# An S5 scan gated by a GEGLU block on one core: up weights loaded in whole rows, the first slab's up products regrouped, and new orders

## The chip, the cores and the metric

The kernel runs on one core of a Trainium2 chip. The metric is the device time of one execution in microseconds, lower is better. Differences of about 0.3% are at the edge of what a measurement of this kernel can tell.

## The reference

The input x has 2048 tokens of 512 features (bfloat16). It is normalized, and the normalized rows go two ways: through a diagonal state space layer with 512 complex states, and through a GEGLU block with 1376 hidden columns.

```python
xn = _layernorm(x)                       # no scale, no shift
# S5
dt = exp(log_dt); Lam_bar = exp(dt * Lam)
B_bar = ((Lam_bar - 1.0) / Lam)[:, None] * Bmat
Bu = einsum("bld,pd->blp", xn, B_bar)
h[t] = Lam_bar * h[t-1] + Bu[t]          # 2048 steps
s = 2.0 * einsum("blp,dp->bld", h, Cmat).real + xn * Dskip
# GEGLU, silu, gate
g = silu((gelu(xn @ w_gate) * (xn @ w_up)) @ w_down)
out = x + s * g
```

## The kernel before

**Tiling.** The tokens are cut into four slabs of 512, each of four tiles (`m`) of 128. The 512 features are four row tiles (`k`) of 128. The 1376 hidden columns are cut into three chunks (`c`): 0 to 512, 512 to 1024 and 1024 to 1376. `wu`, `wg` and `wd` are the three weights in the on-chip buffer, `x_tok` holds all of x, `xna` the four normalized tiles of a slab, and `xnT` two slabs of them transposed.

**Work of a slab.** The up and gate products (for each tile three chunks of each weight, four matmuls to a chunk, one per row tile) accumulate in banks of PSUM; ScalarE (ACT) evicts them, with a gelu for the gate; VectorE (DVE) multiplies the two (`gated`); a transposing DMA (`at_t`) turns the product, and `down_pair` multiplies it with `wd`, 11 matmuls for each tile. For the scan, `half(s, h)` multiplies `BT` with `xnT` (16 matmuls in four groups), ACT evicts into `U`, and DVE rotates (`rot`, `turn`), runs four scans and rotates back into `hst`. `y_tile` multiplies `hst` with `C2` (8 matmuls for each tile, on top of a skip term that ACT puts into the bank first), and DVE applies the gate and adds x. The last tile's y is done in two halves.

**The first slab is special.** No transposing DMA has run yet, so its tiles are centered (`center`), transposed on TensorE (`head_t`, four transposes per tile, a copy by DVE or ACT into `xcT`, which lies in the buffer `W`), and multiplied as they come. `up_rows(m, k, c)` is one matmul of one tile, one row tile and one chunk; `first_w` is a whole group of four; both are scaled by the row's inverse deviation `rs` when ACT evicts them (`out_up`). The seven matmuls of `dummies` stand ahead of it.

**Banks.** There are eight PSUM banks: six of pool "ps" and two of pool "pp". `bank(part)` takes from "pp" if `part` is true. Before the change the third chunk and all of tile 3 go to "pp".

**What sets the order.** Every instruction group is added to a `Plan` as a step with its dependences. `Plan.run` emits the steps in the order of the tuple `ORDER`, and `SLOTS` gives the buffer of each group of a pool. Each engine, and each DMA queue, runs its own instructions in the order of emission. The costs, landing times and due times that appear as numbers in the calls, such as those of `load_x` and `load_w`, were for the planner that wrote `ORDER` and `SLOTS`; in the kernel they do nothing. Almost all DMAs are issued from SP's queue.

**The loads before.** In `ORDER`, the first DMAs on SP are: three x tiles; `wu` row 0 of chunk 0, then of chunk 1; `wu` chunk 2 of all four rows in one load; `wu` row 1 of chunk 1; the fourth x tile; the rest of `wu` in four loads; `wg` in two loads, columns 512 to 1376 first; the second slab of x; the broadcast of `Dskip`; `BT` of the real part, the first `xnT`, `BT` of the imaginary part.

The lines of the profile that matter below: L287 `load_w`, L291 `load_slab`, L296 `load_x`, L314 the loads of `BT`, L328 small memsets, L356 the statistics of a slab, L387 and L400 the transposes of `head_t`, L402 and L391 the copies to `xcT`, L436 the transposing DMA into `xnT`, L462 `up_rows`, L499 `first_w`, L471 and L505 their evictions, L536 the up and gate products of later slabs, L564 `down_pair`, L579 y, L615 BT times xnT, L617 its eviction, L627, L635 and L639 the rotations, L646 the scans, L838 the sums of later slabs, L843 their normalization.

Of the kernel before, what the change touches and what calls it, by code (L numbers as in the profile page):

```python
# [18 lines left out]


ORDER = (
# [24 lines left out]
)  # L46
SLOTS = {
# [4 lines left out]
    ),  # L52
    "pp": (
        0, 1, 0, 1, 0, 1, 0, 1, 0, 0, 0, 1, 0, 1, 0, 1, 0, 1, 0, 1, 1, 0, 1, 0, 1, 1, 1, 0, 0, 0, 0, 1, 1, 0, 1, 0, 1, 0, 1,
    ),
    "U": (
        0, 1, 0, 2, 0, 1, 0, 2,
    ),
    "g2": (
        5, 0, 1, 4, 3, 0, 4, 2, 2, 0, 1, 5, 3, 1, 4, 5,  # L60
    ),
    "at": (
        2, 0, 1, 3, 2, 1, 0, 0, 0, 1, 2, 3, 2, 3, 0, 1,
    ),
    "gtA": (
        0, 0, 1, 1, 0, 1, 0, 1, 1, 0, 0, 0, 1, 1, 0, 0,
    ),
    "gtB": (
        1, 1, 0, 0, 0, 0, 1, 1, 1, 0, 0, 0, 0, 1, 0, 1,
    ),  # L70
    "ubA": (
        0, 1, 0, 0, 1, 1, 1, 0, 0, 0, 1, 1,
    ),
    "ubB": (
        0, 0, 1, 1, 1, 0, 0, 1, 0, 0, 1, 0,
    ),
    "yg": (
        0, 0, 1, 1, 0, 1, 0, 1, 0, 1, 1, 0, 0, 0, 1, 0, 1, 0,
    ),
    "ot": (  # L80
        1, 1, 1, 0, 1, 0, 0, 0, 0, 0, 0, 1, 1, 0, 1, 0, 1,
    ),
    "sk": (
        2, 3, 0, 1, 5, 7, 4, 6, 0, 1, 3, 2, 5, 4, 6, 7,
    ),
    "atT": (
        0, 1, 3, 0, 1, 1, 3, 2, 0, 3, 2, 1, 1, 2, 3, 0,
    ),
}

# [58 lines left out]
def kernel(  # L149
# [18 lines left out]
    P = 128  # L168
    S = 2048
    D = 512  # L170
    F = 1376
    KT = D // P
# [5 lines left out]
    M = TS // P  # L178
# [3 lines left out]
    CH = [(0, 512), (512, 1024), (1024, F)]  # L182
# [6 lines left out]
    V, A, G, T = nc.vector, nc.scalar, nc.gpsimd, nc.tensor  # L189
# [11 lines left out]
    wg = sb("wg", [P, KT, F])  # L201
    wu = sb("wu", [P, KT, F])
# [10 lines left out]
    W2 = CH[1][1]  # L213
# [32 lines left out]
    def bank(part=False):  # L246
        pool = "pp" if part else "ps"
        g, i = pl.group(pool)
        return (pool, g), banks[SIZES["ps"] + i if part else i]
# [9 lines left out]
    def pe(n, cols, emit, reads=(), writes=(), **kw):  # L259
        return pl.add(PE, n * (cols + 6) / 2400.0, emit, reads, writes, lag=0.22, **kw)  # L260
# [23 lines left out]
    def load_w(nm, k0, k1, c0, c1, end, landed):  # L284

        w, r = w_of[nm]
        dma_sp(end, landed, lambda: nc.sync.dma_start(out=w[:, k0:k1, c0:c1], in_=r[:, k0:k1, c0:c1]),  # L287
               [(nm, k, c) for k in range(k0, k1) for c in range(3) if c0 <= CH[c][0] < c1])
# [6 lines left out]
    def load_x(m, end, landed):  # L295
        dma_sp(end, landed, lambda: nc.sync.dma_start(out=x_tok[:, m, :], in_=x_r[:, m, :]), [("x", 0, m)])  # L296

    W1 = CH[0][1]
    load_x(0, 1.12, 2.92)
    load_x(1, 1.59, 3.35)  # L300
    load_x(2, 2.06, 3.75)
    load_w("wu", 0, 1, 0, W1, 2.53, 4.4)
    load_w("wu", 0, 1, W1, W2, 3.0, 4.95)
    load_w("wu", 1, 2, 0, W1, 3.47, 5.5)
    load_w("wu", 1, 2, W1, W2, 3.94, 6.05)
    load_x(3, 4.41, 6.6)
    load_w("wu", 2, 3, 0, W1, 4.88, 7.15)
    load_w("wu", 2, 3, W1, W2, 5.35, 7.7)
    load_w("wu", 3, 4, 0, W2, 5.82, 8.8)
    load_w("wu", 0, KT, W2, F, 6.29, 10.0)  # L310
    load_w("wg", 0, KT, W1, F, 6.76, 12.4)
    load_w("wg", 0, KT, 0, W1, 7.23, 14.0)
    for ri, src in enumerate((A_B_re, A_B_im)):
        dma(SP, 2.0, 3.0, lambda ri=ri, src=src: nc.sync.dma_start_transpose(out=BT[:, ri, :, :], in_=src), writes=[("BT", ri)],  # L314
            after=list(sp_last), svc=TURN)
# [138 lines left out]
    def up_rows(m, k, c):  # L454

        a, b = CH[c]
        if (m, c) not in opened:
            opened[m, c] = bank(m == 3)
        key, ps = opened[m, c]

        def f():
            T.matmul(ps[:], lhsT=xcT[:, k, m * P : (m + 1) * P], rhs=wu[:, k, a:b], start=(k == 0), stop=(k == KT - 1))  # L462
        pe(1, 512, f, [("xcT", m, k // 2), ("wu", k, c)], [key])
        if k == KT - 1:
            out_up(m, c, ps, key)

# [263 lines left out]
    for m in range(1, M):  # L730
        norms = rstd(m, m + 1)
    head_t(1)
    up_rows(0, 0, 0)
    up_rows(0, 0, 1)
    head_t(2)
    for c in range(2):
        up_rows(1, 0, c)
    up_rows(0, 1, 0)
    up_rows(1, 1, 0)
    for c in range(2):  # L740
        up_rows(2, 0, c)
    for m in range(2):
        up_rows(m, 1, 1)
    for c in range(2):
        up_rows(2, 1, c)
    head_t(3)
    for c in range(2):
        for m in range(3):
            up_rows(m, 2, c)
    for k in range(3):  # L750
        for c in range(2):
            up_rows(3, k, c)
    for m in range(M):
        for c in range(2):
            up_rows(m, 3, c)
    for m in range(M):
        first_w("wu", m, 2)
    for m in range(M):
        first_gates(m)
    load_slab(1, after=sp_last)  # L760
# [159 lines left out]
```

## Time and profile before

| | |
|---|---|
| runs of the kernel | 178.75, 178.93, 179.28 us; median 178.93 |
| span of the profiled execution | 176.9 us |
| instructions in it | 2418 |
| HBM read, written | 6.46 MB, 2.10 MB |

Only the span is given of the profiled execution; its time is not among the three runs. The span runs from its first to its last instruction; the runs' median lies 2.03 us above it. The profile counts an engine as busy while one of its instructions executes; matmuls are pipelined, so a displayed matmul duration contains its latency, and the chain of waits gives the slots in which they follow one another. "SPq" is the queue of SyncE's DMA issues, "PEld" the weight loads, which overlap the matmuls. A row of the timeline is: start, length, engine, line, operation, what it writes from what, and how many; in brackets stands how long its engine idled before it and who ended that.

### The profile page before, as it was taken

Reading aid. Unit: us, or ns where it says so; the run is one execution under the profiler, and the core shown is the slowest. Engines: PE = TensorE matmul, PEld = TensorE weight load, DVE = VectorE, ACT = ScalarE, POOL = GpSimd, SP = SyncE. Lnnn points to the kernel's source line nnn. Section 1 sums busy time; section 2 is a strip of 40 time slices with the busy share of each in tenths; the row PEclk is TensorE's granted clock in tenths of the full one; section 3 lists DMA queues with packets and bytes.
Section 4 is the critical chain, followed back from the end, with each engine's and each line's share of the span. In section 5 each row is a group of like instructions: output and inputs, shape, how many; then the busy total and the mean of one; then the engine's idle time right before and its main releaser. Section 6 shows DMA issues by size and latency. Waiting matters only on the chain.

```text
span 176.9 us, 2418 instructions
## 1 busy us (share of the span) xinstructions
PE 172.1 (97%) x834; PEld 82.3 (47%) x849; DVE 154.6 (87%) x253; ACT 132.6 (75%) x246; POOL 10.9 (6%) x25
## 2 busy tenths in 40 slices
PE   8999999999999999999999999999999999999992
PEld 2554544454454444444444444444444444444451
DVE  3743799999999988999999699999999999999343
ACT  6679999989999999956697665735898860793310
POOL 2640500000200000011000000000000000000000
PEclk9999999999999999999999999999999999999999
DMA  5999999997092730040057050063007300550531
GB/s 150 285 347 247 160 288 189 305 217 158 8 193 43 138 62 4 0 82 0 0 115 150 2 111 0 0 126 70 0 11 154 87 0 4 129 123 0 113 119 30
DMA packets 48467, 18.66 MB, mean 105 GB/s; under 512 B 40296, under 2 KB 48328, under 8 KB 48456
## 3 DMA queue, kind: packets, MB, share of 16 engines
q1 hardware_dynamic: 48432, 18.52, 46.7%
q8 instruction: 6, 0.10, 0.2%
q14 instruction: 5, 0.04, 0.1%
q10 hardware_dynamic: 24, 0.00, 0.0%
HBM read 6.46 MB, written 2.10 MB: 48 GB/s over the span
## 4 chain that ended last, share of the span: by engine, by line
PE 94%; DMA 2%; SPq 1%; issue 1%; DVE 0%
PE bank L536 31%; PE bank L564 21%; PE bank L615 16%; PE bank L579 16%; PE bank L499 7%; PE bank L462 3%; DMA wu<-in_B_w_up_dram 2%; SPq L296 1%; SPq L287 0%; DVE yg L585 0%; DVE ot L586 0%; PE bank L400 0%
## 5 line engine op out<-in xcount | busy, mean ns | idle before, releaser
L536 PEld LDWEIGHTS <-xnT 128*128 128x128 bf16 x288 | 28.1, 98 | 29.4
L564 PE MATMUL bank<-wd,atT 128*128 128x512 bf16 (+1 forms) x174 | 40.2, 379 | 0.1
L536 PE MATMUL bank<-wu,xnT 128*128 128x512 bf16 (+1 forms) x140 | 31.9, 356 | 0.1
L536 PE MATMUL bank<-wg,xnT 128*128 128x512 bf16 (+1 forms) x139 | 31.7, 356 | 0.3
L615 PE MATMUL bank<-xnT,BT 128*128 128x512 bf16 x128 | 30.9, 379 | 0.1
L646 DVE TENSOR_TENSOR_SCAN Fs<-rho,ini,W 128x512 bf16<-128x512 f32 x24 | 29.8, 1272 | 0.1
L579 PE MATMUL bank<-C,hst 128*128 128x512 bf16 (+1 forms) x134 | 29.7, 366 | 0.1
L564 PEld LDWEIGHTS <-atT 128*128 128x128 bf16 (+1 forms) x176 | 17.2, 98 | 20.3
L539 ACT ACTIVATE ubA<-bank 128x512 bf16<-128x512 f32 x24 | 14.6, 614 | 8.8 <-PE bank L536 8.3
L617 ACT ACTIVATE U<-bank 128x512 bf16<-128x512 f32 x32 | 19.1, 622 | 1.7 <-PE bank L615 1.7
L579 PEld LDWEIGHTS <-hst 128*128 128x128 bf16 x136 | 13.3, 98 | 14.0
L615 PEld LDWEIGHTS <-BT 128*128 128x128 bf16 x128 | 12.5, 98 | 14.3
L627 DVE TENSOR_TENSOR Q<-U,tab 128x4096 bf16<-128x4096 bf16 x8 | 18.3, 2287 | 0.7 <-ACT tab L715 0.6
L539 ACT ACTIVATE gtA<-bank 128x512 bf16<-128x512 f32 x24 | 14.8, 616 | 5.3 <-PE bank L536 4.6
L627 DVE TENSOR_TENSOR Q<-Fs,tab 128x4096 bf16<-128x4096 bf16 x8 | 18.3, 2285 | 0.1
L567 ACT ACTIVATE g<-bank 128x512 f32<-128x512 f32 x16 | 9.2, 594 | 12.1 <-PE bank L564 12.1
L585 DVE TENSOR_TENSOR yg<-bank,g 128x512 bf16<-128x512 f32 (+1 forms) x17 | 11.1, 655 | 5.0 <-PE bank L579 4.6
L539 ACT ACTIVATE ubB<-bank 128x352 bf16<-128x352 f32 x12 | 5.7, 475 | 6.6 <-PE bank L536 5.5
L838 ACT ACTIVATE junk<-x_tok 128x512 bf16<-128x512 bf16 x16 | 10.2, 649 | 0.0
L499 PE MATMUL bank<-wg,W 128*128 128x512 bf16 (+1 forms) x47 | 9.7, 356 | 0.1
L843 ACT ACTIVATE xna<-x_tok,nb,rs 128x512 bf16<-128x512 bf16 x12 | 9.6, 876 | 0.0
L575 ACT ACTIVATE bank<-sk 128x512 f32<-128x512 bf16 (+1 forms) x17 | 9.5, 577 | 0.1
(121 smaller groups left out, 190.0 us busy)
## 6 DMA issues: line engine op xcount, KB each, us to landing
out_dram<-ot SPq DMA_DIRECT2D x15, 128.0 KB, 1.8
x_tok<-in_A_x_dram SPq DMA_DIRECT2D x3, 512.0 KB, 5.6
wd<-in_B_w_down_dram SPq DMA_DIRECT2D x1, 1280.0 KB, 7.1
wg<-in_B_w_gate_dram SPq DMA_DIRECT2D x1, 864.0 KB
wu<-in_B_w_up_dram SPq DMA_DIRECT2D x6, 128.0 KB, 3.3
x_tok<-in_A_x_dram SPq DMA_DIRECT2D x4, 128.0 KB, 2.2
wg<-in_B_w_gate_dram SPq DMA_DIRECT2D x1, 512.0 KB, 7.8
wu<-in_B_w_up_dram SPq DMA_DIRECT2D x1, 352.0 KB, 3.9
```

The costliest lines, as they stand in the source:

```text
L499: T.matmul(ps[:, 0 : b - a], lhsT=xcT[:, k, m * P : (m + 1) * P], rhs=wt[:, k, a:b], start=(k == 0), stop=(k == KT - 1))
L536: T.matmul(ps[:, 0 : b - a], lhsT=xnT[:, s % 2, m, k, :], rhs=wt[:, k, a:b], start=(k == 0), stop=(k == KT - 1))
L539: acts(b - a, lambda: act(out=dst, in_=ps[:, 0 : b - a], func=AF.Copy if up else AF.Gelu_apprx_tanh), [key], [ok], table=None if up else " ...
L564: T.matmul(ps[:], lhsT=atT[:fs, k, iT * P : (iT + 1) * P], rhs=wd[:fs, k, :], start=(k == 0), stop=(k == NFT - 1))
L579: T.matmul(ps, lhsT=hst[s % 2][:, j // NPT, j % NPT, m * P : (m + 1) * P], rhs=C2[:, j // NPT, j % NPT, c0:c1], start=False, stop=(j == 2 ...
L585: dve(w, lambda: V.tensor_tensor(out=yg[iy][:, 0:w], in0=ps, in1=g2[ig][:, c0:c1], op=ALU.mult), [key, ("g2", gg)], [("yg", gy)])
L615: T.matmul(ps[:], lhsT=BT[:, ri, k, pt * P : (pt + 1) * P], rhs=xnT[:, s % 2, :, k, :], start=(k == 0), stop=(k == KT - 1))
L617: acts(512, lambda q=q, ri=ri, ps=ps: act(out=U[ui][:, ri, q, :], in_=ps[:], func=AF.Copy), [key], [("U", ug, q, ri)])
L627: dve(4096, lambda: V.tensor_tensor(out=Qf, in0=src.unsqueeze(1).to_broadcast(WQ), in1=table, op=ALU.mult), reads, ["Q"], rate=2.0)
L646: pl.add(DVE, 1.12 if s == 0 else 1.185, lambda ri=ri, q=q, pt=pt, first=first: V.tensor_tensor_scan(out=Fs[:, ri, q, :], data0=rho[:, pt ...
L838: acts(512, lambda i=i, fn=fn, sc=sc, m=m: act(out=junk()[:], in_=x_tok[:, s * M + m, :], func=fn, scale=sc, accum_out=sx[:, s, i, m : m + ...
L843: acts(512, lambda m=m: act(out=xn[m], in_=x_tok[:, s * M + m, :], func=AF.Identity, scale=rs[:, s, m : m + 1], bias=nb[:, s, m : m + 1]), ...
```

## The change

Each of the four row tiles of `wu` is loaded whole, 128 rows of 1376 columns, in place of nine pieces, and `wg` in one load in place of two; the x tiles are interleaved with them. The first slab's up products are regrouped: tiles 0 and 1 run all three chunks row tile by row tile, tile 2 its first two chunks in the same way, and tile 2's third chunk and all of tile 3 are groups of four matmuls by `first_w`. Tile 2, not tile 3, now takes the "pp" banks. `up_rows` writes as many columns as the chunk has. `ORDER` and `SLOTS` are new throughout, so every engine's order changes, not only at the head. The numbers of the steps shift as there are fewer loads.

```diff
-    W1 = CH[0][1]
     load_x(0, 1.12, 2.92)
     load_x(1, 1.59, 3.35)
-    load_x(2, 2.06, 3.75)
-    load_w("wu", 0, 1, 0, W1, 2.53, 4.4)
-    load_w("wu", 0, 1, W1, W2, 3.0, 4.95)
-    load_w("wu", 1, 2, 0, W1, 3.47, 5.5)
-    load_w("wu", 1, 2, W1, W2, 3.94, 6.05)
-    load_x(3, 4.41, 6.6)
-    load_w("wu", 2, 3, 0, W1, 4.88, 7.15)
-    load_w("wu", 2, 3, W1, W2, 5.35, 7.7)
-    load_w("wu", 3, 4, 0, W2, 5.82, 8.8)
-    load_w("wu", 0, KT, W2, F, 6.29, 10.0)
-    load_w("wg", 0, KT, W1, F, 6.76, 12.4)
-    load_w("wg", 0, KT, 0, W1, 7.23, 14.0)
+    load_w("wu", 0, 1, 0, F, 2.06, 4.45)
+    load_x(2, 2.53, 4.9)
+    load_w("wu", 1, 2, 0, F, 3.0, 5.95)
+    load_w("wu", 2, 3, 0, F, 3.47, 7.0)
+    load_x(3, 3.94, 7.5)
+    load_w("wu", 3, 4, 0, F, 4.6, 8.5)
+    load_w("wg", 0, KT, 0, F, 5.1, 12.6)
...
-            opened[m, c] = bank(m == 3)
+            opened[m, c] = bank(m == 2)
...
-            T.matmul(ps[:], lhsT=xcT[:, k, m * P : (m + 1) * P], rhs=wu[:, k, a:b], start=(k == 0), stop=(k == KT - 1))
-        pe(1, 512, f, [("xcT", m, k // 2), ("wu", k, c)], [key])
+            T.matmul(ps[:, 0 : b - a], lhsT=xcT[:, k, m * P : (m + 1) * P], rhs=wu[:, k, a:b], start=(k == 0), stop=(k == KT - 1))
+        pe(1, b - a, f, [("xcT", m, k // 2), ("wu", k, c)], [key])
...
     head_t(1)
-    up_rows(0, 0, 0)
-    up_rows(0, 0, 1)
+    for m in range(2):
+        for c in range(3):
+            up_rows(m, 0, c)
     head_t(2)
...
+    for k in range(1, KT):
+        for m in range(2):
+            for c in range(3):
+                up_rows(m, k, c)
+        if k == 1:
+            for c in range(2):
+                up_rows(2, 0, c)
+        for c in range(2):
+            up_rows(2, k, c)
     head_t(3)
...
+    first_w("wu", 2, 2)
+    for c in range(3):
+        first_w("wu", 3, c)
     for m in range(M):
         first_gates(m)
```

The orders themselves, as built, put the following differently. SP issues, after the loads above, the second x slab, the broadcast of `Dskip`, the first `xnT`, `BT` of the imaginary and then of the real part, the third x slab, and the second `xnT`. TensorE starts with tile 0's first and third chunk, the small transposes and tile 0's second chunk; the gate products begin after all up products but four matmuls of tile 2's second chunk and the group of its third. ACT's first up eviction is that of tile 1's third chunk; from its second up eviction to the last of the second slab's normalizations (L843) stand 11 evictions of 512 columns, 5 of 352, a table load, two sines and two small copies. TensorE has six groups of BT before its first product of the second slab. Its last groups are: two of `down_pair`, y of tile 2 and of tile 0, `down_pair`, y of tile 1, `down_pair`, and the two halves of y of tile 3.

More of the change, by code (lines that the diff above doesn't have):

```diff
@@ L48 @@
     "ps": (
[3 rows of a table removed]
[3 rows of a table added]
     ),
     "pp": (
-        0, 1, 0, 1, 0, 1, 0, 1, 0, 0, 0, 1, 0, 1, 0, 1, 0, 1, 0, 1, 1, 0, 1, 0, 1, 1, 1, 0, 0, 0, 0, 1, 1, 0, 1, 0, 1, 0, 1,
+        0, 0, 1, 0, 1, 0, 0, 0, 0, 1, 1, 1, 0, 0, 1, 0, 1, 1, 1, 1, 0, 0, 1, 0, 1, 0, 1, 1, 0, 0, 1, 0, 1, 0, 1, 1, 0,
     ),
     "U": (
-        0, 1, 0, 2, 0, 1, 0, 2,
+        0, 1, 2, 0, 1, 2, 0, 1,
     ),
     "g2": (
-        5, 0, 1, 4, 3, 0, 4, 2, 2, 0, 1, 5, 3, 1, 4, 5,
+        4, 3, 0, 2, 1, 2, 0, 5, 2, 5, 4, 3, 0, 1, 3, 4,
     ),
     "at": (
-        2, 0, 1, 3, 2, 1, 0, 0, 0, 1, 2, 3, 2, 3, 0, 1,
+        2, 0, 1, 3, 0, 2, 0, 3, 2, 3, 1, 3, 0, 1, 3, 2,
     ),
     "gtA": (
-        0, 0, 1, 1, 0, 1, 0, 1, 1, 0, 0, 0, 1, 1, 0, 0,
+        1, 0, 0, 1, 1, 0, 1, 0, 1, 0, 1, 0, 1, 0, 0, 1,
     ),
     "gtB": (
-        1, 1, 0, 0, 0, 0, 1, 1, 1, 0, 0, 0, 0, 1, 0, 1,
+        0, 1, 0, 1, 1, 1, 0, 1, 1, 0, 1, 1, 0, 0, 1, 1,
     ),
     "ubA": (
-        0, 1, 0, 0, 1, 1, 1, 0, 0, 0, 1, 1,
+        0, 1, 0, 1, 1, 0, 1, 0, 0, 1, 1, 0,
     ),
     "ubB": (
-        0, 0, 1, 1, 1, 0, 0, 1, 0, 0, 1, 0,
+        1, 1, 1, 0, 0, 1, 1, 0, 1, 1, 0, 0,
     ),
     "yg": (
-        0, 0, 1, 1, 0, 1, 0, 1, 0, 1, 1, 0, 0, 0, 1, 0, 1, 0,
+        0, 0, 1, 0, 1, 1, 0, 0, 1, 1, 0, 0, 1, 1, 0, 1, 1, 0,
     ),
     "ot": (
-        1, 1, 1, 0, 1, 0, 0, 0, 0, 0, 0, 1, 1, 0, 1, 0, 1,
+        0, 1, 1, 0, 1, 1, 0, 1, 1, 1, 1, 1, 0, 0, 1, 1, 0,
     ),
     "sk": (
-        2, 3, 0, 1, 5, 7, 4, 6, 0, 1, 3, 2, 5, 4, 6, 7,
+        3, 2, 0, 1, 5, 6, 7, 4, 0, 2, 1, 3, 7, 5, 4, 6,
     ),
     "atT": (
-        0, 1, 3, 0, 1, 1, 3, 2, 0, 3, 2, 1, 1, 2, 3, 0,
+        2, 0, 2, 1, 3, 3, 2, 0, 2, 0, 3, 1, 1, 0, 3, 2,
     ),
@@ L732 @@
     head_t(1)
-    up_rows(0, 0, 0)
-    up_rows(0, 0, 1)
+    for m in range(2):
+        for c in range(3):
+            up_rows(m, 0, c)
     head_t(2)
[L736 to L745, printed above, removed]
-    head_t(3)
[L747 to L757, printed above, removed]
+    for k in range(1, KT):
[7 more added lines that the diff above has]
+            up_rows(2, k, c)
+    head_t(3)
+    first_w("wu", 2, 2)
+    for c in range(3):
+        first_w("wu", 3, c)
     for m in range(M):
```

54 rows, old and new, of tables (ORDER, SLOTS) are left out of this document.

## The prediction

> **What bounds the kernel now.** I read the page's busy times, then the table of stretches around the moment at which TensorE stops waiting, then the chain of waits.
>
> ```profile
> span 176.9 us, 2418 instructions
> PE 172.1 (97%) x834; PEld 82.3 (47%) x849; DVE 154.6 (87%) x253; ACT 132.6 (75%) x246; POOL 10.9 (6%) x25
> ```
> ```profile
> 4.84:6.99 2.15, 2.09 (x15) 0.89 (x13) 1.75 (x5) 1.61 (x5) 1.35 (x3) 1.00 1.02 333
> 6.99:173.77 166.78, 165.97 (x807) 80.04 (x821) 150.22 (x233) 127.60 (x233) 8.46 (x14) 1.00 0.47 103
> ```
> ```profile
> 3.06 3.89 DMA wu<-in_B_w_up_dram
> ...
> 6.99 1.35 PE bank L499 x8
> ...
> 10.24 0.22 PE bank L400 x4
> ...
> 12.40 0.60 PE bank L499 x4
> ...
> 29.85 0.86 PE bank L499 x4
> ...
> 164.45 5.18 PE bank L579 x24
> 169.63 2.38 PE bank L564 x11
> 172.01 1.76 PE bank L579 x16
> ```
>
> In a row of stretches the first number after the stretch is its length, the next TensorE's busy time, the last three the granted clock, the DMA engines' share and GB/s. From 6.99 to 173.77 TensorE works 165.97 of 166.78 us at clock 1.00. The chain names one wait of its own before that: the third column chunk of `wu`, 3.89 us under way, lands at 6.95. After it the chain is TensorE's slots alone: 0.86 us for four 512-column matmuls (0.216 each), 0.60 for four of 352 (0.149), 0.22 for four transposes. So the kernel is at TensorE's bound except for its head, and an edit that leaves the matmuls as they are can win only what the head wastes. The head, by TensorE's timeline:
>
> ```profile
> 4.60 0.40 PE L400 MATMUL bank<-ident,xna 128*128 128x128 bf16 x4
> 4.84 0.38 PE L462 MATMUL bank<-wu,W 128*128 128x512 bf16 x1
> 5.21 0.40 PE L400 MATMUL bank<-ident,xna 128*128 128x128 bf16 x4
> 5.54 0.17 PE L672 MATMUL bank<-ident,pv 4*128 4x4 bf16 x1
> 5.67 1.25 PE L462 MATMUL bank<-wu,W 128*128 128x512 bf16 x5
> ```
> ```profile
> 5.07 0.42 DVE L402 COPY W<-bank 128x512 bf16<-128x512 bf16 x1
> ```
>
> A displayed time includes the matmul's latency, so slots are counted: from 4.84 to 6.99 (2.15 us) stand six up matmuls (6 x 0.216 = 1.30), four transposes (0.22) and the two small ones (about 0.10), 1.62 us in all. Idle: 0.53 us. That is the ceiling of the gain, 0.3% of 178.93.
>
> **The change, part by part.** *The matmuls.* Their number and shapes stay; the up products are only regrouped. Cost 0.
>
> *Start of the stream.* The first tile's two transposed halves and the second tile's transposes have the same producers as before, so the first up matmul can stand at 4.84 again if its weights are there. The changed order places 512 and 352 columns of tile 0, the small transposes and another 512 (0.216 + 0.149 + 0.10 + 0.216 = 0.68 us, to 5.52), then tile 1, whose copy out of PSUM ends at 5.49 and released the matmul at 5.67 before. I charge 0.12 us of idle. From there there is work for each row as it lands. Gain 0.53 - 0.12 = 0.41 us; bounds 0 and 0.53.
>
> *The loads.* Nine DMAs replace fourteen ahead of the x slab; SP gives each about 0.47 us (four in 1.93), so SP is 2.35 us earlier, but the bytes are the same and the DMA engines are full.
>
> ```profile
> 2.11 1.93 SPq L287 DMA_DIRECT2D wu<-in_B_w_up_dram  x4
> 2.88 0.49 DVE L414 TENSOR_SCALAR_CACHE_REDUCE yg<-x_tok 128x320 bf16<-128x320 bf16 x1 [1.84 <-DMA x_tok<-in_A_x_dram]
> 2.00:4.00 2.00, 2.00 (x7) 0.56 (x5) 1.00 (x4) 1.22 (x5) 0.00 (x0) 1.00 0.90 259
> 9.20:11.20 2.00, 1.95 (x14) 1.03 (x13) 0.99 (x6) 1.73 (x5) 0.76 (x3) 1.00 0.97 334
> 12.70:14.20 1.50, 1.50 (x10) 0.74 (x8) 0.00 (x0) 1.31 (x4) 0.00 (x0) 1.00 1.09 385
> ```
>
> The rate of rows of 2752 bytes is not in the trace. Bounds: 259 GB/s (128 KB loads paced by SP) and 385 (a 512 KB load). I take 334, the stretch in which `wg` in rows of 1728 bytes runs, the nearest row. The first x tile lands at 2.88, the second 0.47 later, at 3.35, and then bytes over rate: row 0 of `wu` (0.36 MB) at 4.43, needed at 4.84; row 1 (after an x tile) at 5.90, needed at 6.2; row 2 at 6.98, needed at 7.4; row 3 at 8.45, needed at 9.2; `wg` (1.44 MB) at 12.8, needed at 13.3; the next x slab at 14.3. "Needed" is the sum of slots placed before: up to the first gate product all up matmuls except eight of tile 2 (9.30 - 1.46), eight transposes and the small ones, 8.38 us after 4.96. All hidden, `wg` by 0.5 us only. `wg` in one load is a wait that was not there in this form: behind it stand all gate products on TensorE, and behind these the evictions on ACT.
>
> [...]
>
> *Moved small work.*
>
> ```profile
> 0.91 0.13 DVE L328 MEMSET at<- 128x16 uint32 x3
> ...
> 8.61 0.35 DVE L432 TENSOR_SCALAR xna<-xna,rs 128x512 bf16<-128x512 bf16 x1
> ```
> ```profile
> 16.30 3.03 SPq L436 DMA_TRANSPOSE xnT<-xna  x1
> 19.38 2.42 SPq L314 DMA_TRANSPOSE BT<-in_A_B_im_dram  x1
> ```
>
> Memsets of DVE, an iota of POOL and two transposed loads change places. Three memsets take 0.13 us; two now stand where DVE waits for ACT's sum, four beside the second slab's statistics. 0, hidden by DVE's waits there; bare, under 0.4 us. Both `BT` loads now queue on SP behind the first `xnT`, whose last input DVE has near 13: the fourth tile's transposes end at 9.6, then come its copy, four angle steps and four scalings of about 0.35. With 3.03 and 2.42 us of SP the `BT` half that is used first is issued by 18.5 and needed at 21.4 (slots up to the first BT group). 0.
>
> *The second `xnT`.* This is the wait that I do charge.
>
> ```profile
> 11.41 0.36 ACT L688 ACTIVATE sbt<-ang 128x196 f32<-128x196 f32 x1
> ...
> 12.60 0.30 ACT L697 ACTIVATE sp<-sbt 128x128 bf16<-128x128 f32 x1
> ...
> 15.59 1.28 ACT L505 ACT_TABLE_LOAD   x1
> ...
> 17.47 1.26 ACT L471 ACTIVATE at<-bank,rs 128x512 bf16<-128x512 f32 x2
> 18.61 0.56 ACT L505 ACTIVATE gtB<-bank,rs 128x352 bf16<-128x352 f32 x1
> 19.04 0.70 ACT L471 ACTIVATE at<-bank,rs 128x512 bf16<-128x512 f32 x1
> ...
> 22.94 2.94 ACT L843 ACTIVATE xna<-x_tok,nb,rs 128x512 bf16<-128x512 bf16 x4
> 25.76 0.61 ACT L617 ACTIVATE U<-bank 128x512 bf16<-128x512 f32 x1
> ```
> ```profile
> 25.91 2.98 SPq L436 DMA_TRANSPOSE xnT<-xna  x1
> ```
> ```profile
> DMA to landing us min/median/max: 4.9/5.3/5.8
> ```
>
> The last row is that of the four transposing loads of `xnT`. From start to start ACT takes 0.57 us for a 512-column eviction, 0.43 for 352, 0.705 for an L843. In the changed order ACT is behind from its second up eviction, which TensorE's slots release at 10.7; then come 11 of 512 columns (6.27), 5 of 352 (2.15), the table load, two sines and two copies (about 2.3) and the four L843 (2.82): `xna` is complete at 24.3, against 25.88 before. The transposing DMA lands 4.9 to 5.8 us later: 29.2 to 30.1. TensorE reaches the first product on it after all up and gate work (18.6), eight transposes and the small ones (0.54) and six BT groups (5.18), counted from 4.96: 29.3. Behind that product the whole stream of TensorE is held. Bounds 0 and 0.8; I take 0.3, from the median.
>
> *All later orders.* Matmul slots fill TensorE; the price is any further wait. I take 0, since the nearest rows (6.99 to 173.77 above) show none in an order of the same kind; the rivals bound it.
>
> Sum, on the profiled execution: 176.9 - 0.41 + 0.3 = 176.8. The median of the runs lies 2.03 above that span and so: 178.8.
>
> **Rivals.** *The y tiles of the last slab wait for DVE* (slower). The changed order ends with y, y, down, y, down, y: 3 x 1.73 + 2 x 2.38 + 1.76 = 11.7 us, where the order before had 5.18 + 2.38 + 1.76 = 9.3 after the last state is used first. With TensorE's end at 173.4 the state must be there at 161.7.
>
> ```profile
> 16.14 0.69 DVE L356 BATCH_NORM_STATS2 st<-x_tok 128x6 f32<-128x512 bf16 x1 [4.09 <-DMA x_tok<-in_A_x_dram]
> ...
> 161.69 1.22 DVE L639 TENSOR_TENSOR hst<-Q 128x2048 bf16<-128x2048 bf16 x1
> ```
> ```profile
> DVE sk L445 <- ACT bank L575: 1.5, 1, 1.5
> ```
>
> DVE finished it at 162.9. If it does so again, TensorE waits 1.3 us: 178.93 - 0.41 + 1.3 = 179.8. It decides from the point at which DVE is less than 1.2 us ahead of its old course. For it: DVE is busy 87%, and the set of its work before that state is the same. Against it: it idled 4.1 us for the second x slab (16.1 then, 14.3 now) and 1.5 us behind an ACT copy, which another order need not repeat.
>
> *Rows or `wg` late* (slower). At 259 GB/s `wg` lands at 15.5 and the first gate product waits 2.2 us: 178.93 - 0.41 + 2.2 = 180.7. It decides below about 318 GB/s. Against it: the same engines gave 334 and 385.
>
> *Nothing new waits.* The head gives all it has: 178.93 - 0.53 = 178.4.
>
> **How the numbers follow.** Forecast 178.8: 0.5. y tiles wait, around 179.8: 0.25. Loads late, 179 to 180.7: 0.15. Full gain, 178.4: 0.1. A difference of 0.3% (0.54 us) is about what a measurement can tell here. The ceiling of 0.53 sits at that bound, so faster gets 0.1. Same gets nine tenths of the forecast's 0.5 and a quarter to a third of each slow rival, 0.56; the rest, 0.34, is slower. The range for 8 in 10 runs from 178.3, the ceiling less the spread of a median, to 180.4, most of the way to the late loads. The forecast's own range is 178.4 to 179.3.
>
> **What would show it.** Right: the chain's only DMA wait on `wu` at the start is gone and up matmuls run without pause from about 4.9; `wg` lands before 13.3; idle of at most 0.8 us at the first product on the second `xnT` near 29.3; otherwise the chain is TensorE alone to its last group, which ends at 173.2 to 173.8. The first rival shows as a wait of the last slab's first y group for DVE near 161.7; the second as gaps of TensorE between 6 and 14 that end with a DMA. Wrong would be a gain above 0.6 us, which needs fewer or faster matmul slots, or a loss from a place that I priced at 0: an accumulation bank that ACT frees late between 22 and 35, where its queue is full.

## The result, and the profile after

The changed kernel takes 180.31 us (median of 4 runs, 179.88 to 181.22) where the kernel before takes 178.93: ratio 1.0077, 95% interval 1.0048 to 1.0106. A later series on another occasion gave 180.16 (6 runs, 179.80 to 181.71) against 178.89, ratio 1.0083 (1.0051 to 1.0116). So it is slower by 1.3 to 1.4 us, outside the 0.54 us that a measurement cannot tell from nothing, where I forecast no change. Its runs also spread more: 1.9 us, against 0.8 of the kernel before in that series. (In the five later series together the kernel before has three single long runs of 87, at 180.4 to 180.8, and the others up to 179.6.)

The profiled execution of the changed kernel took 179.88 us. Its page begins:

```profile
span 178.1 us, 2416 instructions
PE 172.5 (97%) x833; PEld 82.4 (46%) x849; DVE 155.1 (87%) x253; ACT 135.7 (76%) x248; POOL 11.4 (6%) x25
```

The table of stretches puts the difference in place (first the stretch and its length, then TensorE's busy time):

```profile
5.06:14.09 9.03, 8.77 (x49) 4.26 (x50) 5.35 (x19) 7.31 (x18) 4.92 (x13) 1.00 0.97 326
14.09:33.09 19.00, 18.65 (x91) 9.01 (x94) 16.05 (x48) 18.67 (x38) 2.62 (x4) 1.00 1.04 193
33.09:174.53 141.44, 140.75 (x679) 67.54 (x691) 131.37 (x176) 106.70 (x188) 3.22 (x2) 1.00 0.36 78
```

From 33.09 us on the 0.7 us that are missing of busy time are thirteen single matmul records which the trace lacks, one in some 10 us as in the trace before, each showing 0.05 us; no wait stands behind them. So TensorE loses nothing behind 33 us, and the first rival (y tiles waiting for DVE) did not come. What TensorE loses lies ahead of 33 us. TensorE's timeline there (in brackets the idle time before a row, and what ended it):

```profile
4.41 0.60 PE L394 MATMUL bank<-ident,xna 128*128 128x128 bf16 x4
5.06 0.67 PE L456 MATMUL bank<-wu,W 128*128 128x512 bf16 x2
...
13.51 0.38 PE L456 MATMUL bank<-wu,W 128*128 128x512 bf16 x1
14.09 2.12 PE L493 MATMUL bank<-wg,W 128*128 128x512 bf16 x9 [0.20 <-DMA wg<-in_B_w_gate_dram]
...
29.23 1.03 PE L609 MATMUL bank<-xnT,BT 128*128 128x512 bf16 x4
30.09 1.03 PE L530 MATMUL bank<-wg,xnT 128*128 128x512 bf16 x4
30.95 1.03 PE L530 MATMUL bank<-wu,xnT 128*128 128x512 bf16 x4
31.82 1.03 PE L530 MATMUL bank<-wg,xnT 128*128 128x512 bf16 x3
33.09 2.48 PE L530 MATMUL bank<-wu,xnT 128*128 128x512 bf16 x12 [0.24 <-ACT U L611]
```

Counted from start to start, with slots of 0.216 us, three idle times stand in it: 0.2 us ahead of the first up product, which waits for row 0 of `wu`; 0.37 ahead of the first gate product (`wg`); 0.40 ahead of 33.09 (the row before it has four matmuls, one record is missing), where an up product waits for an accumulation bank until ACT has copied an old U group out of it. The first two up products, from 5.06 on, also run slower than that and take 0.24 us more. At the second `xnT` (30.09) it does not wait in this execution. The first two waits are DMA, and the chain of waits names both ends of this stretch:

```profile
1.64 3.38 DMA wu<-in_B_w_up_dram
...
9.90 1.10 PE bank L394 x4
11.02 0.16 ACT at L465
...
29.34 0.74 ACT junk L824 x2
30.07 0.97 ACT U L611 x2
31.05 0.61 ACT junk L824 x2
31.66 0.89 ACT gtB L499 x2
32.55 0.50 ACT U L611
33.04 0.04 issue
33.09 2.48 PE bank L530 x12
```

Before, the chain was TensorE alone from 6.99 us on. Now it runs through ACT and DVE from 11 to 33 us: TensorE arrives late from the head, and behind it ACT's queue is full to the last eviction. One more wait was not in the forecast at all. The list of waits of SP's own queue (total, times, longest) has

```profile
SPq L287 <- DMA wu<-in_B_w_up_dram: 1.0, 1, 1.0
```

SP holds its load of row 3 until row 0 has landed, so row 3 and `wg` are issued 1.0 us later than SP could.

TensorE's last matmul starts 0.83 us later than before (174.31 against 173.48), but the span is 1.2 us longer. The rest lies behind the last instruction of DVE. It is this one, first before, then now:

```profile
174.25 0.29 DVE ot L586
```
```profile
175.08 0.29 DVE ot L580
```

It ends 2.38 us ahead of the end of the span before, and 2.73 now: 0.35 us. In both traces SP ends the program with six waits for landings, some 0.06 us from one to the next where the landing is there already. Before, the landing of the last store is what the last of the six waits for, 0.8 us, to 176.1; now it is what the first waits for, 1.2 us, to 177.0, and the other five come behind it, to 177.3. In the profiles this time goes with the number of DMAs: 64 before, 59 now (`wu` comes in four loads in place of eight, `wg` in one in place of two), and in those below it is 2.45 us with 63 DMAs, 2.63 with 60 and 2.71 to 2.73 with 59, and one of the latter is `before_loads_new`, which has the old order. So this part comes with the loads, whatever the order.

### The profile page after: what moved, and what is told of

The parts are those of the page before. It is cut to its first block, busy times and chain, and to the rows that moved or that the text cites. A ratio compares the mean times of both kernels' runs of the same rounds, so it can differ in the third digit from the quotient of the medians.

```text
span 178.1 us, 2416 instructions
## 1 busy us (share of the span) xinstructions
PE 172.5 (97%) x833; PEld 82.4 (46%) x849; DVE 155.1 (87%) x253; ACT 135.7 (76%) x248; POOL 11.4 (6%) x25
## 4 chain that ended last, share of the span: by engine, by line
PE 82%; ACT 8%; DVE 5%; DMA 2%; issue 1%; SPq 0%
PE bank L530 30%; PE bank L558 21%; PE bank L573 16%; PE bank L609 13%; ACT at L465 3%; PE bank L456 3%; DVE Q L702 2%; DMA wu<-in_B_w_up_dram 2%; ACT gtA L499 1%; DVE at L512 1%; ACT U L611 1%; ACT junk L824 1%; ACT gtB L499 1%; PE bank L394 1%; ACT L499 1%
## 5 line engine op out<-in xcount | busy, mean ns | idle before, releaser
L611 ACT ACTIVATE U<-bank 128x512 bf16<-128x512 f32 x32 | 18.6, 618 | 5.4 <-PE bank L609 5.1
L573 PEld LDWEIGHTS <-hst 128*128 128x128 bf16 x136 | 13.3, 98 | 14.2
L493 PE MATMUL bank<-wg,W 128*128 128x512 bf16 (+1 forms) x47 | 10.2, 357 | 0.3 <-DMA wg<-in_B_w_gate_dram 0.2
```

The costliest lines, as they stand in the source:

```text
L493: T.matmul(ps[:, 0 : b - a], lhsT=xcT[:, k, m * P : (m + 1) * P], rhs=wt[:, k, a:b], start=(k == 0), stop=(k == KT - 1))
L573: T.matmul(ps, lhsT=hst[s % 2][:, j // NPT, j % NPT, m * P : (m + 1) * P], rhs=C2[:, j // NPT, j % NPT, c0:c1], start=False, stop=(j == 2 ...
L611: acts(512, lambda q=q, ri=ri, ps=ps: act(out=U[ui][:, ri, q, :], in_=ps[:], func=AF.Copy), [key], [("U", ug, q, ri)])
```

## The experiments

**1. The same kernel again, and two simple theories apart.** From the profile above two causes could carry the loss: loads that land late (L), or ACT's queue between 11 and 33 us (A). Four kernels on one chip: the changed kernel again; `wg` in two parts,

```diff
-    load_w("wg", 0, KT, 0, F, 5.1, 12.6)
...
+            for c0, c1 in ((0, 512), (512, F)):
+                nc.sync.dma_start(out=w[:, :, c0:c1], in_=r[:, :, c0:c1])
```

three of ACT's sums of slab 2 put off (ACT's own steps of `ORDER`); and both.

```diff
-    182, 133, 293, 131, 103, 141, 139, 297, 176, 180, 294, 119, 143, 201, 178, 308, 295, 353, 296, 195, 292,
+    182, 133, 131, 103, 141, 139, 176, 180, 119, 143, 201, 178, 308, 295, 353, 296, 195, 293, 297, 294, 292,
```

> The changed kernel once more, unchanged, for its level and spread beside the variants. Both theories: 180.0 to 180.5 us, and in the profile three idle places of TensorE: the first up matmul near 5.06 (row 0 of wu lands late), about 0.4 us before the first gate product near 14.1 (wg), and about 0.4 us before the fourth product of the second slab near 33.1 (a bank that ACT frees late).

> w_gate loaded in two pieces, columns 0 to 512 of all rows first; the order is that of the changed kernel. Theory L (the late loads set the loss): the wait before the first gate product goes and the time falls by 0.3 to 0.4 us, to about 179.9. Theory A (ACT's queue from 11 to 33 us sets it): the wait before the gate product goes, but the wait for the bank near 33 grows by as much, to about 0.8 us, and the time stays at 180.2 to 180.4.

> Three of the third slab's sums on ACT (L824, 0.6 us each with their readout) are moved in ORDER from ahead of the last evictions of the first half's U to behind them; nothing else changes. Theory A: the U evictions come 1.8 us earlier, the wait for the bank near 33 goes, and the time falls by about 0.4 us, to 179.9. Theory L: that wait was only a consequence; the time stays within 0.15 us of the changed kernel.

> Both edits together. Theory A and theory L: both waits go; if the loss sits in these two places the time falls by 0.7 to 0.8 us against the changed kernel, to about 179.5, and what is left above the kernel before (178.9) is the late start and something later than 33 us. If the time stays above 180, the loss lies elsewhere.

Measured: 180.16, 180.57 (179.67 to 181.69), 180.84 (180.22 to 182.49) and 180.66 us (180.28 to 182.17). None is faster. In the profile of `wg_two` the wait for `wg` is gone, and yet its first gate product starts at 14.13, no sooner than 14.09. Something ahead of it holds the head. The repeated changed kernel shows what, on TensorE's timeline:

```profile
5.20 0.53 PE L456 MATMUL bank<-wu,W 128*128 128x512 bf16 x2 [0.34 <-DMA wu<-in_B_w_up_dram]
...
5.79 0.97 PE L456 MATMUL bank<-wu,W 128*128 128x512 bf16 x4
7.51 0.96 PE L456 MATMUL bank<-wu,W 128*128 128x352 bf16 x4 [0.75 <-DMA wu<-in_B_w_up_dram]
...
30.98 1.04 PE L530 MATMUL bank<-wg,xnT 128*128 128x512 bf16 x4 [0.25 <-DMA xnT<-xna]
```

Row 1 of `wu` arrives just before 7.51, and TensorE idles 0.92 us for it. The list of DMA issues (kilobytes, us from issue to landing) for that row, first in the changed kernel's first profile, then in this one:

```profile
wu<-in_B_w_up_dram SPq DMA_DIRECT2D x1, 344.0 KB, 3.6
```
```profile
wu<-in_B_w_up_dram SPq DMA_DIRECT2D x1, 344.0 KB, 4.9
```

It is issued at 2.6 us in both, by the same instructions, and lands at 6.2 in one and at 7.5 in the other. Over the eleven profiles that load `wu` in this way in the new order, row 0 lands at 4.7 to 5.5 and row 1 at 6.2 to 7.5, with 7.0 in the middle. In the middle the same profile waits 0.41 us for the second `xnT`, not for a bank. In `sums_later` the bank is free in time, but the wait moves to that `xnT` (0.49 us) and two new ones come at 40.6 and 42.4, 0.22 and 0.42 us, behind the sums that were put off. So both theories had hold of something, and each edit uncovered the next wait.

**2. One part at a time.** Row 0 of `wu` in two loads, columns 0 to 512 first; two matmuls on constants ahead of the first up product; two ACT steps moved in the middle (127, tile 1's gtB eviction, behind the four `xna`; 293, a sum, behind the U evictions); and the kernel before with whole row 0 alone:

```diff
-    load_w("wu", 0, 1, 0, F, 2.06, 4.45)
...
+            for c0, c1 in zip(cuts, cuts[1:]):
+                nc.sync.dma_start(out=w[:, k : k + 1, c0:c1], in_=r[:, k : k + 1, c0:c1])
```
```diff
         def f():
+            if (m, k, c) == (0, 0, 0):
+                for _ in range(2):
+                    T.matmul(ps[:, 0:256], lhsT=warm[:, 0:P], rhs=warm[:, 0:256], start=True, stop=True)
```
```diff
-    240, 127, 153, 242, 239, 241, 182, 133, 293, 131, ... 201, 178, 308, 295,
+    240, 153, 242, 239, 241, 127, 182, 133, 131, ... 201, 178, 293, 308, 295,
```
```diff
-    load_w("wu", 0, 1, 0, W1, 2.53, 4.4)
-    load_w("wu", 0, 1, W1, W2, 3.0, 4.95)
+    load_w("wu", 0, 1, 0, F, 2.53, 4.4)
+    dma_sp(3.0, 4.95, lambda: None, [])
...
-    load_w("wu", 0, KT, W2, F, 6.29, 10.0)
+    load_w("wu", 1, KT, W2, F, 6.29, 10.0)
```

> The changed kernel with wu's first row tile loaded in two parts, columns 0 to 512 ahead of the rest, within the same step; the order of everything is untouched. Theory H (the head: TensorE idles before its first up product because that product waits for a whole row tile, and the idle also keeps its matmuls at the slow rate, 427 ns in place of 216 ns, for up to some us more; rows that land late differ from run to run): the first up product starts by about 4.8 us where the profiles of the changed order had 5.06 to 5.54, the idle of 0.2 to 0.7 us ahead of it goes, and the median falls by 0.3 to 0.8 us, to 179.4 to 179.9, with fewer runs above 181. Theory M (the middle: the loss is the 0.3 to 0.5 us wait near 31 us for the second xnT or for a bank that ScalarE frees, and what follows it): within 0.2 us of the changed kernel's 180.2.

> The changed kernel with two matmuls of 256 columns on constants put ahead of the first up product, into the bank which that product then starts anew; they need no data, and take 0.11 us each at the full rate and 0.21 at the slow one. Theory H with the rate (the idle before the first up product is what keeps the matmuls slow): TensorE is busy without a gap up to the first up product, the products from there on take 216 ns, no run is above 180.8, and the median falls by 0.2 to 0.6 us, to about 179.8. Theory H without the rate (only the waiting for rows counts): the dummies lie in the wait, and the median is within 0.2 us of the changed kernel's 180.2, with as wide a spread. Theory M: the same, 180.2 to 180.4.

> The changed kernel with two ScalarE steps moved: tile 1's gtB eviction behind the four xna, so that the second xnT is turned about 0.45 us sooner, and one sum of slab 2 (0.63 us) behind the U eviction that frees the bank, where ScalarE had a gap. Theory M: the wait near 31 to 33 us goes, whichever of the two it was, and the median falls by 0.3 to 0.5 us, to about 179.8, with the spread as before. Theory H: the wait goes too, but the head still differs between runs by over 1 us, so the highest run stays above 181 and the median stays above 179.6. If the work only queues up later: 180.2, with a new wait near 40 us.

> The kernel before, in its own order, with one part of the change alone: wu's first row tile loaded whole (1376 columns) in one load where it loaded 512 and 512 columns, and the load of the last 352 columns left with three rows. Theory H: the first up product starts near 5.2 us in place of 4.84, the idle ahead of it grows by 0.3 to 0.5 us, and the median rises by 0.3 to 1.2 us over the kernel before, to 179.2 to 180.1, with a wider spread. Theory M, and any theory by which the new orders alone set the loss: within 0.2 us of the kernel before, 178.9.

Measured: `row0_cut` 180.64 (180.07 to 181.55), a miss: the first product starts at 5.03, but its third chunk then waits for the second part of the row until 6.38. The first 512 columns land at 3.85, in time, and the other 864 at 6.33, later than the whole row does; and its matmuls stay slow to 9.4 (below), so its time is not the price of the cut alone. `dummies_gap` 180.20 (179.76 to 181.73): in its profile the matmuls already ran at the full rate when the constants came, so it says little. `mid_order` 179.73 (179.38 to 179.88), ratio to the kernel before 1.0043 (1.0029 to 1.0057), against 1.0083 of the changed kernel: theory M's 0.4 us are there, and half (by the ratios) to two thirds (by the medians) of the loss are left. `before_row0_whole` 179.19, but nine runs at 178.90 to 179.65 and three at 181.19 to 181.25. Its profile is of one of the three:

```profile
4.57 0.61 PE L400 MATMUL bank<-ident,xna 128*128 128x128 bf16 x4
5.59 0.59 PE L462 MATMUL bank<-wu,W 128*128 128x512 bf16 x1 [0.42 <-DMA wu<-in_B_w_up_dram]
...
6.68 2.31 PE L462 MATMUL bank<-wu,W 128*128 128x512 bf16 x5
```

Five matmuls of 512 columns take 2.31 us, 0.43 each, where the kernel before has 1.25 for five at 5.67. This goes on to 9.96 us, and the granted clock of the profile shows 1.00 all the while. Matmuls start at that half rate in every profile. In fifteen of all nineteen profiles the full rate comes between 3.4 and 6.6 us. In the other four (`before_row0_whole`, `before_loads_new`, `row0_cut`, `sums_later`) it comes at 9.4 to 10.0, and these four have 0.5 to 0.9 us of idle between 4.8 and 6.4 while the rate was low; none of the fifteen has, if two are read as at the edge: in `only_sum` an idle of 0.8 us begins at 4.4, and the full rate is there when it ends at 5.25; in `wg_two_sums_later` one of 0.7 us begins at 4.85, just as the transposes ahead of it pass to the full rate. So a late full rate goes with an idle at the low rate in these profiles: 9.4 to 10.0 us with one, 3.4 to 6.6 without. That the idle is the cause, as theory H has it, was my estimate; no run here moves the idle alone to show it, and no trace shows what sets the moment.

**3. What is left: landing or rate.** `mid_order` again as a base; with three such matmuls on constants; with 128 KB of tokens loaded between row 0 and x tile 2, which nobody needs yet; and `before_row0_whole` with the three constants.

```diff
-    load_x(2, 2.53, 4.9)
...
+        nc.sync.dma_start(out=x_tok[:, 15, :], in_=x_r[:, 15, :])
+        nc.sync.dma_start(out=x_tok[:, 2, :], in_=x_r[:, 2, :])
```

> The kernel of mid_order once more, as the base of two others on this chip. Theory M for the middle: 179.6 to 179.9 again, against 180.2 of the changed kernel. If the 179.73 was a lucky head: 180.0 or more, and single runs above 181.

> mid_order with three matmuls of 256 columns on constants ahead of the first up product (0.11 us each at the full rate, 0.21 us at the slow one). Theory R (idle of TensorE ahead of the first up product is what leaves the matmuls at the slow rate for some us more): the median falls by 0.1 to 0.4 us from mid_order's, and no run lies over 180.3. Theory L (what is left of the loss is the landing of wu's row tiles, whatever the rate of TensorE): within 0.15 us of mid_order, or up to 0.2 us slower.

> mid_order with one load more, between wu's first row tile and x tile 2: 128 KB of tokens that are not needed until slab 3 (loaded again there). It delays wu's row tiles 1 to 3 and wg by 128 KB at the 270 GB/s of the first 15 us, 0.47 us, and nothing else. Theory L (the rows' landing sets the head): the median rises by 0.3 to 0.6 us over mid_order's. If the rows have slack behind the slow matmuls: under 0.15 us.

> The kernel before_row0_whole (the kernel before with wu's first row tile loaded whole: median 179.19, 3 of 12 runs at 181.2, where its profile shows matmuls at the slow rate until past 9.6 us behind an idle of 0.58 us) with three matmuls of 256 columns on constants ahead of the first up product, to fill that idle. Theory R: the runs at 181.2 are gone; all lie between 178.8 and 179.7. If the slow stretch has another cause than the idle: some 1 in 4 runs stay at 181 or more.

Measured: 179.83 (179.24 to 180.79), 179.68 (179.05 to 180.05), 180.28 (180.01 to 181.26), and 179.31 (178.90 to 179.62, 11 runs). 128 KB in the way cost 0.45 us, about the time that these bytes take (0.43 us at the 308 GB/s that `mid_order` moved from 3.35 to 7.20 us): the rows have no slack. The constants take no more than 0.15 us off the median of `mid_order`; what they may take off is the long runs: one of eight at 180.8 without them and none of eight with them here, three of twelve at 181.2 and none of eleven in `before_row0_whole`, where in the profile five up matmuls take 1.25 us again. These are few runs, and `dummies_gap`, with two constants, still had one at 181.73. The two profiles of `mid_order` happen to have the one and the other form of the head. The first:

```profile
4.90 0.92 PE L456 MATMUL bank<-wu,W 128*128 128x512 bf16 x2
...
5.90 2.25 PE L456 MATMUL bank<-wu,W 128*128 128x512 bf16 x8
...
14.31 1.03 PE L493 MATMUL bank<-wg,W 128*128 128x512 bf16 x4
```

and the second:

```profile
4.76 0.53 PE L456 MATMUL bank<-wu,W 128*128 128x512 bf16 x2
...
5.35 0.97 PE L456 MATMUL bank<-wu,W 128*128 128x512 bf16 x4
7.20 0.96 PE L456 MATMUL bank<-wu,W 128*128 128x352 bf16 x4 [0.88 <-DMA wu<-in_B_w_up_dram]
...
14.32 1.03 PE L493 MATMUL bank<-wg,W 128*128 128x512 bf16 x4
```

One is slow to 6.5 us and idles only 0.23 us for row 1 (ahead of 7.20, inside its last row of up products); the other has the full rate by 4.5 us and idles 1.04 us for it. Both begin the gate products within 0.01 us of each other: the landing of row 1, 7.2 us in both, sets the head, and the slow rate merely fills the wait unless it goes on past it.

**4. Taking bytes away, and the loads without the order.** Row 1 ahead of x tile 2, without and with the constants; and all of the new loads in the old order:

```diff
-    load_x(2, 2.53, 4.9)
-    load_w("wu", 1, 2, 0, F, 3.0, 5.95)
+    load_w("wu", 1, 2, 0, F, 2.53, 5.6)
+    load_x(2, 3.0, 5.95)
```
```diff
+    load_w("wu", 0, 1, 0, F, 2.53, 4.4)
...
+    load_w("wu", 1, 2, 0, F, 3.47, 5.5)
...
     load_x(3, 4.41, 6.6)
...
+    load_w("wu", 2, 3, 0, F, 4.88, 7.15)
...
+    load_w("wu", 3, 4, 0, F, 5.82, 8.8)
...
+    load_w("wg", 0, KT, 0, F, 6.76, 12.4)
```

> mid_order with wu's second row tile loaded ahead of x tile 2 in place of behind it: 128 KB less ahead of the row tile that TensorE waited 1.04 us for in a profile of mid_order. Theory L (the landing of that row tile sets the head): it lands 0.3 to 0.5 us sooner, x tile 2 comes later by 1.0 us but is wanted only after four products of that row, and the median falls by 0.2 to 0.4 us, to 179.4 to 179.6. If the rows have slack, or tile 2 becomes the late one: 179.8 or more.

> The same with three matmuls of 256 columns on constants ahead of the first up product. Theory L with R as a tail: the median is within 0.2 us of mid_x2_later, and no run lies over 180.1. It would have to be under 178.9 to beat the kernel before: expected by none.

> The kernel before, in its own order, with all of the change's loads: each up row tile whole, w_gate in one load (x tile 2 ahead of the first row tile, as before). Theory L, by which whole rows land too late for what the order asks of them (1.3 us of products for each row tile of 344 KB in this order, 1.16 us in the new one): 179.3 to 180.3, with some runs at 181 where an idle leaves the matmuls slow. If the loads alone cost nothing and the new order makes the whole loss: within 0.2 us of the kernel before, 178.9.

Measured: 180.49 (180.13 to 181.16), 180.24 (179.42 to 180.78) and 181.50 (181.21 to 183.02). All three are misses of the time: 179.4 to 179.6 was expected of the first, no run over 180.1 of the second, 179.3 to 180.3 of the third. The first is no miss of the head: row 1 lands at 5.91, 1.25 us sooner than in `mid_order`, though the 128 KB that no longer stand ahead of it are only 0.45 us by `mid_more_bytes`. TensorE's timeline of `mid_x2_later`:

```profile
13.87 3.35 PE L493 MATMUL bank<-wg,W 128*128 128x512 bf16 x16
...
22.86 0.82 PE L609 MATMUL bank<-xnT,BT 128*128 128x512 bf16 x3 [0.78 <-DMA BT<-in_A_B_im_dram]
```

The gate products begin 0.44 us sooner than in `mid_order`, and 0.94 us are lost at 22.86, where TensorE waits for `BT`. SP's timeline says why, first `mid_order`, then `mid_x2_later`:

```profile
13.59 1.98 SPq L430 DMA_TRANSPOSE xnT<-xna  x1
15.62 3.93 SPq L308 DMA_TRANSPOSE BT<-in_A_B_im_dram  x1
```
```profile
14.05 2.02 SPq L430 DMA_TRANSPOSE xnT<-xna  x1
16.12 3.73 SPq L308 DMA_TRANSPOSE BT<-in_A_B_im_dram  x1
```

In the new order both `BT` loads stand behind the first `xnT`, and this waits for the x tiles to be normalized: x tile 2 later makes the `xnT` 0.46 us later. From the issue of the first `xnT` to the first product on `BT` it is 8.7 to 9.0 us in the profiles of the new order (13.25 and 22.15 in the changed kernel), so `BT` comes in step with it. So the new order has two chains that end together near 22.3: rows to TensorE, and x tiles to `xnT` to `BT`. What relieves the one at the other's cost gains nothing. `before_loads_new` shows that the old order is worse served still by whole rows: its first product waits to 5.52, its matmuls stay slow to 9.6, its gate products begin at 17.17 where they began at 15.00. How much of these 2.2 us is the late row and how much the slow rate that went with it, this one profile doesn't separate.

**5. Which of the two middle waits.** Each half of the edit of `mid_order` alone: step 127 moved (`only_xna`), step 293 moved (`only_sum`).

> The changed kernel with one half of mid_order: tile 1's gtB eviction behind the four xna, nothing else. Theory B (either wait comes up when the other is gone): the wait for the bank stays, 0.3 to 0.4 us near 32 to 33 us, and the median is 180.0 to 180.2, that of the changed kernel. If the second xnT was the whole of it: 179.8.

> The changed kernel with the other half of mid_order: one sum of slab 2 behind the U evictions, nothing else. Theory B: the bank is free in time and the wait for the second xnT stays, 0.2 to 0.5 us near 30 to 32 us; the median is 180.0 to 180.2. If the bank was the whole of it: 179.8.

Measured: 180.34 (179.81 to 181.52) and 180.17 (179.61 to 181.49), ratios 1.0078 (1.0051 to 1.0104) and 1.0057 (1.0028 to 1.0086). `only_xna` alone gains nothing on the changed kernel's 1.0077 and 1.0083. For `only_sum` the times don't decide: its median is above the 179.73 and 179.83 of both, but the kernel before was at 179.16 in this series, and its ratio is that of `mid_order_again`. In the profile of `only_xna` the bank is late again:

```profile
33.61 1.24 PE L530 MATMUL bank<-wu,xnT 128*128 128x512 bf16 x5 [0.23 <-ACT U L611]
```

That is 0.40 us from start to start, as in the changed kernel, and another 0.34 us stands ahead of 28.30, where a bank waits for a gate eviction. In that of `only_sum` no wait stands there, but its head was 0.6 us late (gate products at 14.89), which hides one. So the profile of `only_xna` shows that the bank's wait comes up when that for `xnT` is eased. That the wait for `xnT` comes up when the bank is free is shown by `sums_later` above, in a run with a slow head, and not by `only_sum`.

## Why the prediction was wrong

*What bounds the kernel, and the ceiling*: right. No run of the changed kernel is faster than any of the kernel before beside it; from 33 us to its last matmul TensorE alone sets the time, and the later orders cost it nothing, as priced. The end of the program was not in the sum: the 0.35 us behind the last DVE instruction were put at nothing without a reason.

*Start of the stream* (0.12 us of idle charged, gain 0.41): the step failed, because row 0 was put at 4.43, in time for 4.84, and lands at 4.7 to 5.5.

*The loads* (0, all hidden): this is the step that made the prediction wrong. I let every row land at bytes over 334 GB/s from 3.35 us on, as if the loads came one behind the other and each was there as soon as its bytes fitted. Row 1 was to land at 5.90 and was needed at 6.2; it lands at 6.2 at best and at 7.0 in the middle of the eleven profiles, at 7.2 in both of `mid_order`, and 7.2 less 6.2 is the 1.0 us by which TensorE waits in the second of these. The first gate product, by my sum of slots due at 13.3, begins at 14.1 to 14.6 in nine of the eleven, at 14.3 in the middle one, and in the other two at 14.9 and 15.8. The rate itself was nearly right, by the table of stretches of `mid_order` (the last number is GB/s):

```profile
0.00:6.20 6.20, 5.41 (x20) 1.96 (x21) 2.29 (x11) 3.98 (x10) 0.69 (x6) 1.00 0.67 196
3.35:7.20 3.85, 3.76 (x19) 1.41 (x17) 2.04 (x10) 3.02 (x8) 0.34 (x2) 1.00 0.95 308
```

At 308 GB/s my sum gives 6.1 for row 1, and by 6.2 us 1.2 MB had moved, more than the 1.10 MB of the three x tiles and rows 0 and 1 (a row is 0.352 MB, where I took 0.36). Yet row 1 lands at 7.16, when 1.5 MB had moved: some 0.4 MB of them belong to loads that were issued behind it. So the step that failed is the landing, not the rate; why a load lands a microsecond after its bytes would have fitted stays open. The trace before had the same, and I read over it: by my sum the third `wu` load there would land at 5.6, and its row in the chain of waits (3.06, 3.89 us under way) says 6.95. The sign that I had named for it, "gaps of TensorE between 6 and 14 that end with a DMA", is what the profiles show; it had a chance of 0.15. That rival was priced on the average rate to `wg`; it came through row 1, half as large, by a landing that differs from run to run. SP's wait for row 0 was missed too; row 3, the load behind it, was the late one in `only_sum` (0.84 us of idle ahead of 10.76) and in `wg_two_sums_later` (0.19 ahead of 10.10).

*The `BT` loads behind the first `xnT`* (0): the place was right, the working was not. I took the time of issue, "by 18.5", for the one that counts. SP's timeline of the changed kernel, and its two times from issue to landing:

```profile
13.25 3.00 SPq L430 DMA_TRANSPOSE xnT<-xna  x1
16.29 2.37 SPq L308 DMA_TRANSPOSE BT<-in_A_B_im_dram  x1
18.70 2.76 SPq L308 DMA_TRANSPOSE BT<-in_A_B_re_dram  x1
```
```profile
DMA to landing us min/median/max: 5.4/5.8/6.3
```

The half used first, from 22.15 on, is that with 5.4: it lands at 21.7, later than the 21.4 at which I needed it. It costs nothing in the first profile of the changed kernel, since TensorE is later too, and is the wall behind the rows.

*The second `xnT`* (0.3 charged, bounds 0 and 0.8): right in place and mechanism, small in size. `mid_order`, which removes this wait and the bank's, gains 0.3 to 0.4 us (180.16 to 179.83 and 179.73, in three series). The bank that ACT frees late, which I priced at 0 and named as what might prove me wrong, is part of it: 0.40 us in the first profile. The two share one price, since TensorE pays only the later of them.

*The sum*: 178.8, plus 1.0 for the head (14.3 less 13.3), plus 0.1 for the middle (0.4 less 0.3), plus 0.35 for the end gives 180.25, beside the 180.31 and 180.16 measured. In the first profile the same three places give 0.8, 0.1 and 0.35, 1.25 of the 1.3 us by which its span of 178.1 exceeds my 176.8. What the half rate adds to single long runs of the changed kernel is not separated by a run.

*Rival 1, the y tiles*: not seen; TensorE has no wait near 162 us. *That nothing new waits*: refuted.

No version here beats the kernel before. The best of the new order, `mid_order` with the constants, is at 179.68, ratio 1.0046 (1.0029 to 1.0064). The kernel before asks for 1024 columns of a row in its first passes, 256 KB for 1.3 us of products; the new order asks for 344 KB for 1.16 us, about 300 GB/s from the first row on. From 3.35 to 7.20 us the engines moved 300 to 350 GB/s in the eleven profiles, and the x tiles had to come out of that too.

## What to carry to other kernels

Price a load in the head by a landing in the trace, from issue to landing, and not by its bytes over a rate: here the rate was right to a tenth and the landing wrong by a microsecond. Then compare bytes asked for with microseconds of work that they feed. Where an order is rebuilt, look for chains that end at the same time: several experiments here that shortened one met the next, and of the two small waits in the middle easing that for `xnT` alone paid nothing. Compare the two ends of the program as well, from the last instruction of an engine to the end of the span. Where a loss is a fraction of a per cent, one profile is one draw: the same loads landed 1.3 us apart.

## What the hardware showed that I had not expected

- The same load, issued at the same time behind the same others, landed at 6.2 us in one execution and at 7.5 in another, in the first 8 us of the program. In `mid_order` it landed a microsecond after the bytes up to its end would have fitted at the rate of that stretch, 308 GB/s.
- Matmuls of 512 columns take 0.43 us at first and 0.216 later, while the granted clock of the profile reads 1.00 for both. The full rate comes between 3.4 and 6.6 us in fifteen profiles, and at 9.4 to 10.0 us in the four with an idle of 0.5 to 0.9 us while the rate was low. One of these four is of a run at 181.2 us of a kernel whose other runs but two lie at 178.9 to 179.7.
- The time from the end of the last DVE instruction to the end of the span is 2.38 us with 64 DMAs in the program and 2.71 to 2.73 with 59. Of the six landings that SP waits for at the end, that of the last store is the last in the profile with 64 and the first in the one of the changed kernel.
- SP held its eighth load in the queue for 1.0 us until an earlier one had landed, though it had nothing else to wait for.
- Cutting a late load in two brought a part sooner and the whole later: with row 0 in two parts the first landed at 3.85 us and the second at 6.3, where the whole row lands at 4.7 to 5.5.
